# A whole planned order of 4654 tasks rewritten, with the planner's durations changed, in a fused dynamic-convolution and gated-FFN kernel on one core

## The chip, the core and the metric

The kernel runs on one core of one Trainium2 chip. The metric is the device time of one execution in microseconds (us). Beside it stands the profile of one execution: each engine's instructions with their start, length and what released them. The engines are PE (TensorE, matmul; its weight loads are listed apart as PEld), DVE (VectorE), ACT (ScalarE), POOL (GpSimd) and SP (SyncE, which here only issues DMAs). L616 means line 616 of the kernel.

## What is computed

```python
# x: (4, 4160, 192) f32; weight_gen: (4, 4160, 8, 7) f32
w = softmax(weight_gen, axis=-1)                       # 8 heads, 7 taps
a[b, s, h, g] = sum_k w[b, s, h, k] * x_pad[b, s + k, h, g]   # the 7 rows up to s, 24 columns a head
# gated FFN, d_ff = 1024
h = relu(a @ w_in)
c = cw[0] * h[s - 1] + cw[1] * h[s] + cw[2] * h[s + 1]
out = (h * sigmoid(c)) @ w_out
```

## The kernel before

The 16640 rows of the sequence lie as 128 segments of 130 rows, one segment on each of the 128 partitions. The kernel works in 33 blocks of R = 4 rows of every segment. A block goes through these steps, and the names are those of the profile:

- **Products.** POOL multiplies rows of x (tile `ring`) by the softmax weights (tile `w`, two blocks to a group), one tap at a time (L511): four taps into a `px` buffer, three into a `py` buffer. There are three px and two py buffers, used in turn, so block q uses px number q mod 3 and py number q mod 2. In blocks 0 to 2 (PLAN "a") a few products of block 0 are DVE's and TensorE sums all seven products while it transposes them (L554, L565).
- **Folds.** From block 3 on (REST, "d") the products are summed in three steps: `fold1` (L527) is an accumulating DMA that adds the three py pieces to three px pieces, `fold2` (L530) an accumulating DMA that adds px pieces 2, 3 to 0, 1, and `fold3` (L537) a pair of POOL additions of the last two. POOL issues the two DMAs and both use POOL's DMA queue.
- **Softmax of a weight group:** maximum (L447, DVE), subtraction (L450, POOL), exp (L453, ACT), sum (L456, DVE), reciprocal (L465, DVE), product (L472, POOL).
- **Transposes and split.** TensorE transposes the sum (L565), ACT writes its rounded part (`H`, L589), DVE the rest (`L`, and the lower half of `H2`, L593); a small SP transfer copies `H2` to `HB` (L582).
- **Eight units** of 128 of the 1024 hidden columns each: nine matmuls into a PSUM bank `z` (L616), relu (L627, ACT), middle tap of the convolution (L631, ACT), the side taps (L638, DVE, two of them), tanh (L645, ACT), gate product `g` (L654, DVE). ACT carries two rows to the next block (L659).
- **Second matmul** (L675, two blocks later), evacuation (L682, ACT) and store (L686, SP).

Every matmul uses 64 of TensorE's 128 rows; the lower and the upper half work side by side and are planned as two engines, P0 and P8. At the start the weights have to be decoded from f64 bit patterns: chunk by chunk, ACT (L339, L342), four DVE steps (L346, L349, L352, L357), ACT (L860) and DVE (L865), then SP transfers the folded rows (`spread`, L879).

What sets the order: the program first writes down all tasks as (engine, duration, dependences), then takes ORDER, a permutation of the 4654 task numbers, and computes for each task in that order the earliest start that the model allows:

```python
for i in order:
    best[i] = max([best[d] + l_ for d, l_ in preds[i]] + [free.get(u, 0.0) for u in uses[i]] + [0.0])
    for u in uses[i]:
        free[u] = best[i] + dur[i]
seq = [i for i in sorted(range(nt), key=lambda i: (best[i], pos[i])) if tasks[i][3] is not None]
```

The instructions are emitted by rising `best`, so the durations and ORDER together decide only in which order each engine gets its instructions. At run time an engine takes them strictly in that order, and semaphores hold each back until its data are there. Both DMA folds occupy a modelled resource "D" (`dadd`).

Of the kernel before, what the change touches and what calls it, by code (L numbers as in the profile page):

```python
# [36 lines left out]
T_X = (7.4, 11.1)  # L37
T_W = (3.5, 9.5)
# [4 lines left out]
    ("f", 0, 256, 8.2, "VGP", "G"),  # L43
    ("m", 0, 256, 9.0, "VVP", "G"),
    ("f", 256, 512, 11.9, "GVP", "V"),
    ("m", 256, 512, 12.3, "VVP", "G"),
# [225 lines left out]
def kernel(  # L272
# [24 lines left out]
    R = 4  # L297
# [394 lines left out]
    with tc.manual_schedule():  # L692
# [151 lines left out]
        def used(ix):  # L844
            return [k for i in ix for k in last_use[i]]
# [45 lines left out]
        for q in range(2, WB):  # L891
            softmax(q, dma(0.5, spreads[q - 2:q - 1], lambda q=q: load_w(q)))
# [264 lines left out]
```

## Time and profile before

| | us |
|---|---|
| median of 3 runs (lowest, highest) | 695.01 (694.62, 695.83) |
| the profiled execution's own time | 695.11 |
| its span, first to last instruction | 693.4 |
| PE busy | 671.6 |
| DVE busy | 625.2 |
| ACT busy | 610.3 |
| POOL busy | 512.9 |

1.7 us of the profiled execution lie outside its span. A busy TensorE is not TensorE at its peak: its "busy" is the union of both halves, so a stretch in which one half works counts whole, and so does one at half clock. The number of matmuls in a stretch tells more.

### The profile page before, as it was taken

The page shows a single profiled execution, that of the slowest core. Times are in us where ns is not written, and L with a number is a line of the kernel's source. Part 1 is how long each engine was busy: PE and PEld are TensorE (multiplying, and loading weights), DVE is VectorE, ACT ScalarE, POOL GpSimd, SP SyncE. Part 2 cuts the span into 40 slices and gives each one's busy share as a digit, 9 for nine tenths or more (in the row PEclk, how much of TensorE's full clock was granted, in tenths as well). Part 3 has the DMA queues.
Part 4 walks back from the last instruction along what each step waited for, and adds up shares of the span by engine and source line. Part 5 has one row for each costly group of instructions (what it writes and reads, how often), then busy time and mean ns, then how long its engine had stood idle before and what let it go on. Part 6 is the DMA issues. An engine that isn't in the chain of part 4 may idle for free.

```text
span 693.4 us, 17805 instructions
## 1 busy us (share of the span) xinstructions
PE 671.6 (97%) x7177; PEld 652.6 (94%) x7177; DVE 625.2 (90%) x998; ACT 610.3 (88%) x1216; POOL 512.9 (74%) x417
## 2 busy tenths in 40 slices
PE   4899979999999999999999999999999999999998
PEld 3789979999999999999999999999999999999997
DVE  7699968999999999999999999999989998999982
ACT  4489969999999999999999999999999999899972
POOL 6899977989997886959888995798886984731000
PEclk9699989999999999999999999999999999999999
DMA  8728757797888877467977867579858775470101
GB/s 247 212 69 167 160 124 148 157 210 138 181 167 177 165 154 140 97 148 167 202 157 161 182 139 143 111 167 181 183 109 167 138 146 106 89 149 32 33 24 46
DMA packets 38634, 98.79 MB, mean 142 GB/s; under 512 B 3534, under 2 KB 8269, under 8 KB 38552
## 3 DMA queue, kind: packets, MB, share of 16 engines
q0 software_dynamic: 20192, 59.01, 48.6%
q1 hardware_dynamic: 18042, 38.19, 17.4%
q8 instruction: 56, 0.92, 0.5%
q10 hardware_dynamic: 318, 0.46, 0.3%
q14 instruction: 26, 0.21, 0.1%
HBM read 20.51 MB, written 12.78 MB: 48 GB/s over the span
## 4 chain that ended last, share of the span: by engine, by line
PE 80%; POOL 12%; DMA 3%; issue 2%; ACT 1%; DVE 1%; SPq 0%; ACTq 0%; DVEq 0%; POOLq 0%
PE ops L675 39%; PE z L616 36%; POOL px L511 5%; POOL py L511 4%; DMA px<-px 2%; PE tp L565 2%; PE z L675 1%; POOL px L537 1%; POOL px L530 1%; DMA stage<-in_moe_w_in_dram 1%; PE ops L554 1%; POOL w L472 1%; POOL px L527 0%; PE tp L675 0%; PE tp L554 0%
## 5 line engine op out<-in xcount | busy, mean ns | idle before, releaser
L675 PE MATMUL ops<-wo,g 64*128 64x192 f32 x4032 | 575.7, 326 | 0.0
L675 PEld LDWEIGHTS ops<-wo,g 64*128 64x128 f32 x4032 | 537.8, 187 | 6.6 <-ACT o L682 2.5
L616 PE MATMUL z<-H,wi 64*128 64x512 f32 x1716 | 477.6, 425 | 0.5 <-DVE g L654 0.2
L638 DVE SCALAR_TENSOR_TENSOR z<-h,cw,z 128x512 f32<-128x512 f32 (+1 forms) x528 | 379.3, 741 | 24.2 <-ACT z L631 16.8
L616 PEld LDWEIGHTS z<-H,wi 64*128 64x128 f32 x1716 | 292.1, 188 | 5.4 <-DVE g L654 2.2
L511 POOL TENSOR_TENSOR px<-ring,w 128x768 f32<-128x768 f32 (+1 forms) x145 | 234.4, 1870 | 25.7 <-PE tp L565 21.7
L616 PE MATMUL z<-L,wi 64*128 64x512 f32 x528 | 201.9, 395 | 0.0
L654 DVE SCALAR_TENSOR_TENSOR g<-z,h 128x512 f32<-128x512 f32 (+1 forms) x264 | 173.9, 676 | 13.2 <-ACT z L645 11.0
L631 ACT ACTIVATE z<-h,cw 128x512 f32<-128x512 f32 (+1 forms) x264 | 180.4, 685 | 4.5
L627 ACT ACTIVATE h<-z 128x512 f32<-128x512 f32 x264 | 156.7, 595 | 25.8 <-PE z L616 20.5
L511 POOL TENSOR_TENSOR py<-ring,w 128x768 f32<-128x768 f32 (+2 forms) x108 | 167.3, 1759 | 0.0
L645 ACT ACTIVATE z<-z 128x512 f32<-128x512 f32 (+1 forms) x264 | 148.5, 574 | 6.0 <-DVE z L638 5.1
L537 POOL TENSOR_TENSOR px<-px 128x512 f32<-128x512 f32 (+1 forms) x60 | 69.2, 1341 | 46.3 <-DMA px<-px 46.1
L616 PEld LDWEIGHTS z<-L,wi 64*128 64x128 f32 x528 | 97.0, 186 | 1.3
L659 ACT ACTIVATE h<-h 128x512 f32<-128x512 f32 x128 | 79.2, 623 | 0.0
L565 PEld LDWEIGHTS tp<-ident,px 64*128 64x128 f32 x424 | 46.5, 145 | 11.2 <-POOL px L537 6.0
L565 PE MATMUL tp<-ident,px 64*128 64x64 f32 x424 | 49.3, 230 | 7.8 <-POOL px L537 5.1
L589 ACT ACTIVATE H<-tp 64x256 fp32r<-64x256 f32 (+1 forms) x93 | 42.2, 453 | 12.2 <-PE tp L565 8.8
L616 PE MATMUL z<-HB,wi 64*128 64x512 f32 x132 | 52.1, 394 | 0.0
L530 POOL DMA_DIRECT2D px<-px x30 | 42.3, 1409 | 12.5 <-DMA px<-py 12.2
L682 ACT ACTIVATE o<-ops 128x192 f32<-128x192 f32 x126 | 40.8, 323 | 10.5 <-PE ops L675 9.9
L527 POOL DMA_DIRECT2D px<-py x30 | 46.1, 1538 | 4.5 <-POOL py L511 4.5
(80 smaller groups left out, 293.1 us busy)
## 6 DMA issues: line engine op xcount, KB each, us to landing
px<-py POOLq DMA_DIRECT2D x30, 1152.0 KB, 9.9
px<-px POOLq DMA_DIRECT2D x30, 768.0 KB, 7.0
ring<-in_x_dram SPq DMA_DIRECT2D x31, 384.0 KB, 6.2
out_dram<-o SPq DMA_DIRECT2D x31, 384.0 KB, 5.1
HB<-H SPq DMA_DIRECT2D x33, 128.0 KB, 3.0
w<-in_weight_gen_dram SPq DMA_DIRECT2D x15, 224.0 KB, 6.4
r_out<-in_moe_w_out_dram SPq DMA_DIRECT2D x4, 384.0 KB, 4.8
wi<-scr SPq DMA_DIRECT2D x8, 128.0 KB, 5.3
```

Source lines behind the costliest of these rows:

```text
L511: eng.tensor_tensor(out=dst[:, a:b, :].rearrange("p s (h g) -> p s h g", g=GRP), in0=ring[:, p:p + n, :].rearrange("p s (h g) -> p s h g", ...
L530: nc.gpsimd.dma_start(out=fl4(px_b[q % NX][:, 0:2]), in_=fl4(px_b[q % NX][:, 2:4]), accum_op=ALU.add, max_dma_last_dim=3072)
L537: nc.gpsimd.tensor_tensor(out=dst.rearrange("p (s d) -> p s d", s=R), in0=a[:, :, lo:hi], in1=b[:, :, lo:hi], op=ALU.add)
L565: return nc.tensor.matmul(dst[0:D2 if part and i >= 0 else P, c * P + s * H2_:c * P + (s + 1) * H2_], lhsT=src, rhs=ident[r, r], is_transp ...
L616: return [lambda i=i, w=w, nm=nm: nc.tensor.matmul(out=z, lhsT=w[:, fs], rhs=h_t[j, nm][r], start=(not s and i == 0), stop=(s == 1 and i = ...
L627: nc.scalar.activation(out=hrow(f, 2, R), in_=rows(z_t[j, f]), func=ACTF.Relu)
L631: nc.scalar.activation(out=rows(z_t[j, f][:, :no * P]), in_=hrow(f, cc, no), func=ACTF.Copy, scale=cw[:, NF + f:NF + f + 1])
L638: nc.vector.scalar_tensor_tensor(out=z, in0=hrow(f, cc + d, no), scalar=cw[:, k * NF + f:k * NF + f + 1], in1=z, op0=ALU.mult, op1=ALU.add,)
L645: nc.scalar.activation(out=z, in_=z, func=ACTF.Tanh, scale=0.5)
L654: nc.vector.scalar_tensor_tensor(out=rows(g_of(j, f)), in0=rows(z_t[j, f][:, :no * P]), scalar=1.0, in1=hrow(f, cc, no), op0=ALU.add, op1= ...
L659: nc.scalar.activation(out=h[:, f0 // CG, 0:2].rearrange("p s f t -> p (s f t)"), in_=h[:, f0 // CG, R:R + 2].rearrange("p s f t -> p (s f ...
L675: return nc.tensor.matmul(out=hold[0][2][:, 0:D], lhsT=g_of(j, n)[r, c], rhs=wo[r, n, :], start=(first and n == 0), stop=(last and n == NF ...
```

## The change

ORDER is replaced as a whole. The modelled durations and landing times change with it: first arrivals of x and w (T_X, T_W), arrivals of the weight chunks (CH), issue times and landing times of loads and stores, POOL's time to issue a fold, transposes, splits and the matmul step. No instruction's work changes, and no buffer.

```diff
-T_X = (7.4, 11.1)
-T_W = (3.5, 9.5)
+T_X = (8.2, 11.7)
+T_W = (3.5, 10.3)
...
-    ("f", 0, 256, 8.2, "VGP", "G"),
-    ("m", 0, 256, 9.0, "VVP", "G"),
-    ("f", 256, 512, 11.9, "GVP", "V"),
-    ("m", 256, 512, 12.3, "VVP", "G"),
+    ("f", 0, 256, 9.2, "VGP", "G"),
+    ("m", 0, 256, 9.8, "VVP", "G"),
+    ("f", 256, 512, 13.1, "GVP", "V"),
+    ("m", 256, 512, 14.3, "VVP", "G"),
...
-    "0 1 6 15 24 33 44 53 64 384 4 385 2 5 3 7 8 9 10 11 12 13 14 25 27 131 28 132 133 34 29 26 36 35 134 30 148 37 "
...
-        m_late = dma(0.5, [], lambda: load_in(nc.sync, *CH[4][:3]))
-        x_t_[2] = dma(0.5, [], lambda: load_x(2 * R - 1, 2 * R + 3))
+        m_late = dma(2.3, [], lambda: load_in(nc.sync, *CH[4][:3]))
+        x_t_[2] = dma(1.8, [], lambda: load_x(2 * R - 1, 2 * R + 3), 4.5)
...
-            softmax(q, dma(0.5, spreads[q - 2:q - 1], lambda q=q: load_w(q)))
+            softmax(q, dma(1.0, spreads[q - 2:q - 1], lambda q=q: load_w(q), 4.5))
...
-                x_t_[q] = dma(1.2, all_taps.get(q - RB, []), lambda: load_x(R * q - 1, R * q + 3), 8.0)
+                x_t_[q] = dma(1.8, all_taps.get(q - RB, []), lambda: load_x(R * q - 1, R * q + 3), 8.0)
...
-                a_ = dadd([prod[i] for i in (0, 1, 2, 4, 5, 6)], 6.5, lambda: fold1(q), 0.82)
+                a_ = dadd([prod[i] for i in (0, 1, 2, 4, 5, 6)], 6.5, lambda: fold1(q), 1.3)
...
-                    a_ = dadd([a_, prod[3]], 4.4, lambda: fold2(q), 0.775)
+                    a_ = dadd([a_, prod[3]], 4.4, lambda: fold2(q), 1.0)
...
-                            f_ = task("P8" if s else "P0", 0.06 * nc_, [e_] + after,
-                                      [(0.06, lambda n=n, c=c, s=s, one=one: one(n, c, s)) for c in range(nc_)])
+                            f_ = task("P8" if s else "P0", 0.07 * nc_, [e_] + after,
+                                      [(0.07, lambda n=n, c=c, s=s, one=one: one(n, c, s)) for c in range(nc_)])
...
-                a_ = task("A", 0.56 if pr else 0.49, [f_] + hd, lambda part=part, pr=pr: split_hi(q, part, hold[part], pr))
-                l_ = task("V", 0.78 if pr else 0.6, [a_], lambda part=part, pr=pr: split_lo(q, part, hold[part], pr))
+                a_ = task("A", 0.74 if pr else 0.49, [f_] + hd, lambda part=part, pr=pr: split_hi(q, part, hold[part], pr))
+                l_ = task("V", 0.89 if pr else 0.6, [a_], lambda part=part, pr=pr: split_lo(q, part, hold[part], pr))
...
-                stored.append(dma(1.2, [e_], lambda: store(j, 0, no)))
+                stored.append(dma(1.8, [e_], lambda: store(j, 0, no)))
```

What the new table does to the engines' orders is seen in three places.

**First place: POOL, the folds of blocks 4 and 5.** px1 belongs to block 4, px2 and py1 to block 5, px0 to block 6 (and, in fold3, still to block 3). Before:

```order
L537 TENSOR_TENSOR px0_95<-px0_95 128x256
L511 TENSOR_TENSOR py1_99<-ring_82,w3_90 128x768 x2
L527 DMA px2_97<-py1_99 128x3x768
L530 DMA px1_96<-px1_96 128x2x768
L511 TENSOR_TENSOR px2_97<-ring_82,w3_90 128x768
L450 TENSOR_TENSOR w0_87<-w0_87,m0_91 128x448
L450 TENSOR_TENSOR w1_88<-w1_88,m1_93 128x448
L511 TENSOR_TENSOR px0_95<-ring_82,w3_90 128x768 x3
L537 TENSOR_TENSOR px1_96<-px1_96 128x512
```

With the change:

```order
L537 TENSOR_TENSOR px0_95<-px0_95 128x256
L511 TENSOR_TENSOR px2_97<-ring_82,w3_90 128x192
L511 TENSOR_TENSOR px2_97<-ring_82,w3_90 128x576
L511 TENSOR_TENSOR px2_97<-ring_82,w3_90 128x768
L511 TENSOR_TENSOR py1_99<-ring_82,w3_90 128x768
L530 DMA px1_96<-px1_96 128x2x768
L511 TENSOR_TENSOR py1_99<-ring_82,w3_90 128x768 x2
L527 DMA px2_97<-py1_99 128x3x768
L511 TENSOR_TENSOR px2_97<-ring_82,w3_90 128x768
L511 TENSOR_TENSOR px0_95<-ring_82,w3_90 128x768
L537 TENSOR_TENSOR px1_96<-px1_96 128x512
```

fold2 of block 4 (L530 on px1) stood behind fold1 of block 5 (L527 on px2) and now stands ahead of it, with two products between them; the two subtractions L450 of the weight groups 4 and 5 have gone forward, to either side of fold1 of block 4. The next two pairs (blocks 5 and 6, 6 and 7) are exchanged in the same way; the two after them already stood so before.

**Second place: DVE at the start.** dps_224 and dps_228 are the second weight chunk, dps_274 and dps_276 the third, tp and ops the transposed block 0. Before:

```order
L511 TENSOR_TENSOR px0_95<-ring_82,z1_109 128x768
L357 ISA dps_224<-dps_224,scr1_114 128x512
L865 TENSOR_TENSOR wi_79<-dps_224,wi_79 128x256
L346 TENSOR_SCALAR dps_274<-dps_274 128x256
L349 TENSOR_SCALAR scr0_113<-dps_274 128x256
L352 SCALAR_TENSOR_TENSOR dps_274<-dps_274,scr0_113 128x256
L357 ISA dps_274<-dps_274,scr0_113 128x512
L593 TENSOR_TENSOR L1_0_101<-tp_190,H1_0_100 128x512
L865 TENSOR_TENSOR scr0_113<-dps_274,scr0_113 128x256
L593 TENSOR_TENSOR H2_0_102<-ops_176,H2_0_102 64x512
```

With the change:

```order
L511 TENSOR_TENSOR px0_95<-ring_82,z1_109 128x768
L349 TENSOR_SCALAR scr1_114<-dps_228 128x256
L352 SCALAR_TENSOR_TENSOR dps_228<-dps_228,scr1_114 128x256
L357 ISA dps_228<-dps_228,scr1_114 128x512
L593 TENSOR_TENSOR L1_0_101<-tp_190,H1_0_100 128x512
L865 TENSOR_TENSOR wi_79<-dps_228,wi_79 128x256
L593 TENSOR_TENSOR H2_0_102<-ops_179,H2_0_102 64x512
L346 TENSOR_SCALAR dps_276<-dps_276 128x256
```

Both splits (L593) of block 0 now stand ahead of the four decode steps of the third chunk; before they stood behind them.

**Third place: TensorE, the first unit.** tp_190 and ops_ are the banks of block 0, tp_289 and tp_281 that of block 1, z1 the bank of the first unit. Before:

```order
L554 MATMUL tp_190<-ident_76,px0_95 128x128 x4
L565 MATMUL tp_289<-ident_76,px1_96 128x64 x12
L565 MATMUL ops_312<-ident_76,px1_96 64x64
L616 MATMUL z1_109<-H1_0_100,wi_79 128x512
L565 MATMUL ops_312<-ident_76,px1_96 64x64 x3
L616 MATMUL z1_109<-H1_0_100,wi_79 128x512
```

With the change:

```order
L554 MATMUL ops_179<-ident_76,px0_95 64x128 x4
L565 MATMUL tp_281<-ident_76,px1_96 128x64 x4
L616 MATMUL z1_109<-H1_0_100,wi_79 128x512 x2
L616 MATMUL z1_109<-H2_0_102,wi_79 128x512 x2
L616 MATMUL z1_109<-L1_0_101,wi_79 128x512
L565 MATMUL tp_281<-ident_76,px1_96 128x64 x3
```

The first unit's matmuls start behind four transposes of block 1 in place of thirteen. In block 0 the transposes into the `tp` bank now end ahead of those into the `ops` bank.

## Rows read from the trace of the kernel before

**Rows 1.** Two lines of the page's 40 slices: busy tenths, granted clock in tenths
```profile
PE   4899979999999999999999999999999999999998
...
PEclk9699989999999999999999999999999999999999
```

**Rows 2.** Windows: length; PE, PEld, DVE, ACT, POOL busy (instructions); clock, DMA
```profile
80.00:100.00 20.00, 15.64 (x157) 15.09 (x155) 14.67 (x24) 14.41 (x29) 15.28 (x13) 0.90 0.71 145
240.00:260.00 20.00, 20.00 (x223) 19.83 (x221) 19.20 (x31) 18.77 (x39) 16.34 (x13) 1.00 0.67 137
```

**Rows 3.** Waits of TensorE: for whom, us in total, times, longest
```profile
PE tp L565 <- POOL px L537: 5.1, 2, 4.4
PE tp L565 <- DVE L L593: 2.7, 1, 2.7
```

**Rows 4.** Windows of 4 us, same columns
```profile
24.00:28.00 4.00, 4.00 (x31) 3.13 (x31) 0.95 (x2) 1.21 (x3) 4.00 (x4) 0.50 0.67 185
52.00:56.00 4.00, 3.91 (x30) 3.32 (x28) 3.97 (x9) 3.94 (x9) 4.00 (x4) 1.00 0.88 202
92.00:96.00 4.00, 0.53 (x5) 0.23 (x3) 3.18 (x5) 2.22 (x5) 0.43 (x1) 0.98 0.87 221
96.00:100.00 4.00, 3.11 (x24) 3.02 (x25) 0.34 (x1) 0.97 (x2) 4.00 (x4) 0.50 0.14 55
100.00:104.00 4.00, 4.00 (x34) 3.85 (x32) 3.65 (x6) 2.84 (x6) 4.00 (x5) 0.67 0.01 2
104.00:108.00 4.00, 4.00 (x46) 4.00 (x44) 2.37 (x5) 3.07 (x7) 4.00 (x5) 1.00 0.89 152
```

**Rows 5.** TensorE's timeline: start, length, instruction, idle time before it and releaser
```profile
21.16 1.19 PE L565 MATMUL tp<-ident,px 64*128 64x64 f32 x9 [2.75 <-DVE L L593]
22.43 0.77 PE L616 MATMUL z<-H,wi 64*128 64x512 f32 x1
...
96.89 0.37 PE L565 MATMUL tp<-ident,px 64*128 64x64 f32 x1 [4.36 <-POOL px L537]
...
140.88 0.27 PE L565 MATMUL tp<-ident,px 64*128 64x64 f32 x1 [0.72 <-POOL px L537]
```

**Rows 6.** POOL's timeline around the folds of blocks 3 to 5
```profile
46.13 0.98 POOL L450 TENSOR_TENSOR w<-w,m 128x448 f32<-128x448 f32 x1
47.06 4.57 POOL L511 TENSOR_TENSOR py<-ring,w 128x768 f32<-128x768 f32 x3
51.94 1.31 POOL L527 DMA_DIRECT2D px<-py  x1 [0.31 <-POOL py L511]
...
66.91 2.23 POOL L527 DMA_DIRECT2D px<-py  x1
...
80.69 1.29 POOL L527 DMA_DIRECT2D px<-py  x1 [0.30 <-POOL py L511]
81.49 1.72 POOL L530 DMA_DIRECT2D px<-px  x1
...
95.57 1.94 POOL L537 TENSOR_TENSOR px<-px 128x512 f32<-128x512 f32 x2 [4.43 <-DMA px<-px]
```

**Rows 7.** DMA issues in 60:64, 66:68, 83:95, 118:130: count, KB each, us to landing
```profile
px<-px POOLq DMA_DIRECT2D x1, 768.0 KB, 7.1
...
px<-py POOLq DMA_DIRECT2D x1, 1152.0 KB, 12.2
...
px<-px POOLq DMA_DIRECT2D x1, 768.0 KB, 14.0
...
px<-px POOLq DMA_DIRECT2D x1, 768.0 KB, 8.7
```

**Rows 8.** DVE's timeline at the start
```profile
18.50 0.43 DVE L346 TENSOR_SCALAR dps<-dps 128x256 f32<-128x256 f32 x1 [0.98 <-ACT dps L339]
...
20.34 0.68 DVE L593 TENSOR_TENSOR L<-tp,H 128x512 fp32r<-128x512 f32 x1
...
28.22 0.49 DVE L638 SCALAR_TENSOR_TENSOR z<-h,cw,z 128x256 f32<-128x256 f32 x1 [2.48 <-ACT z L631]
```

More of the change, by code (lines that the diff above doesn't have):

```diff
@@ L898 @@
                 wo[:, 2 * c:2 * c + 2].rearrange("p c d -> p (c d)").bitcast(I32), r_out[c],
-                slots[iB][:, 0:w], slots[iC][:, 0:w], dma(1.6, spreads, lambda c=c: load_out(c)), used((iB, iC)), WOE[c],
+                slots[iB][:, 0:w], slots[iC][:, 0:w], dma(1.8, spreads, lambda c=c: load_out(c), 4.0), used((iB, iC)), WOE[c],
             )
@@ L918, in loads @@
                 g0 = 2 * (g - WB)
-                softmax(g, dma(0.7, all_taps[g0] + (all_taps[g0 - 1] if g0 else []), lambda: load_w(g), 9.0))
+                softmax(g, dma(1.0, all_taps[g0] + (all_taps[g0 - 1] if g0 else []), lambda: load_w(g), 9.0))
         def head(q):
@@ L994, in unit @@
             k_ = 4 if late(j, f) else 5
-            a_ = task("P0", 0.231 * k_, deps_, (k_, lambda: mm1(j, f, 0)), after=[last_mm[0]] + ([] if n else zfirst))
-            mm[n] = task("P8", 0.231 * (9 - k_), [a_] + (twins[j] if late(j, f) else []), (9 - k_, lambda: mm1(j, f, 1)),
+            a_ = task("P0", 0.233 * k_, deps_, (k_, lambda: mm1(j, f, 0)), after=[last_mm[0]] + ([] if n else zfirst))
+            mm[n] = task("P8", 0.233 * (9 - k_), [a_] + (twins[j] if late(j, f) else []), (9 - k_, lambda: mm1(j, f, 1)),
                          after=[last_mm[1]])
@@ L1097, in one @@
                     return made[n]()
-                ms = [(0.231, lambda n=n, one=one: one(n)) for n in range(fn[0])]
+                ms = [(0.233, lambda n=n, one=one: one(n)) for n in range(fn[0])]
             else:
```

403 rows, old and new, of the table ORDER are left out of this document.

## The prediction, made before the changed kernel ran

> **What bounds the kernel now.** I read the slices of the page first. TensorE is busy in nine tenths or more of nearly every slice, with a hole in the second and third slice and one in the sixth, and the clock line falls at the same places [rows 1]. The windows of 20 us say what "busy" is worth: a steady stretch holds 223 matmuls in 20 us, that is 11.1 a us, with TensorE at 20.00 and DVE at 19.20 of 20 us; the stretch from 80 to 100 us holds only 157 [rows 2]. So from about 104 us to the end the kernel runs at TensorE's own rate, and a new order can win nothing there: TensorE's work is the same. What can be won lies ahead of it.
>
> The waits of TensorE then name two places: one of 4.4 us for POOL's fold3 and one of 2.7 us for DVE's split [rows 3]. The windows of 4 us show what the first costs. From 92 to 104 us they hold 5, 24 and 34 matmuls, where 46 stand in the one behind them, and the clock is 0.50 (1.2 of 2.4 GHz) in 96 to 100 us, 0.67 in the next and full from 104 on [rows 4]. TensorE's timeline has the gap: 4.36 us up to 96.89, released by L537 of POOL, which is fold3 of block 4 [rows 5].
>
> POOL's timeline tells why fold3 is late. fold1 of block 5 is issued at 80.69 and fold2 of block 4 behind it at 81.49; fold3 of block 4 stands for 4.43 us and starts at 95.57 [rows 6]. The DMA table gives that fold2 14.0 us from issue to landing, where a fold2 with none just ahead of it took 7.1 and one later 8.7 [rows 7]. So the wait is a queue: a fold of 768 KB behind one of 1152 KB that nobody needs yet.
>
> At the start DVE does the split of block 0 at 20.34, behind four decode steps that begin at 18.50 [rows 8]; TensorE waits for it up to 21.16, and its first unit begins at 22.43 [rows 5] at half clock (0.50 in the window from 24 us [rows 4]). DVE itself then waits 2.48 us for that unit, up to 28.22 [rows 8], and is full in the 50s (3.97 of 4 us [rows 4]).
>
> **The change, term by term**, against the profiled execution's own 695.1 us (the median of the runs shown is 695.0, so they can stand for each other). A measurement of this kernel can tell about 0.2%, 1.4 us, from no change.
>
> *Folds of blocks 4 and 5.* When does fold2 of block 4 land now? Before, 81.49 − 51.94 = 29.55 us lay between the issues of fold1 of block 3 and fold2 of block 4, all of it POOL's own work but for 0.3 us of waiting [rows 6]. By the new order two products (4.57 / 3 = 1.5 us each) and the issue of fold1 of block 5 (81.49 − 80.69 = 0.8, with 0.3 idle ahead) leave this stretch, and two subtractions of 0.98 come in: 29.55 − 3.0 − 1.1 + 2.0 = 27.4. So fold2 is issued at 51.94 + 27.4 = 79.3, or a little earlier if POOL gets to block 3 sooner. It lands 7.1 to 8.7 us later, at 86.4 to 88.0, and fold3 (1.94) ends at 88.3 to 89.9, in place of 97.5. fold1 of block 4 has to land first: before it was issued at 66.91, and one subtraction more and two short products less ahead of it leave it about there, 12.4 us ahead of fold2; its landing took 12.2 [rows 7], so it is just there in time. TensorE ran out of work 4.36 us before 96.89, at 92.5. The cover is 2.6 to 4.2 us, and the gap closes. At the dear end fold2 takes 14.0 in its new place too: it lands at 93.3, fold3 ends at 95.2, and a gap of 2.7 us stays.
>
> What the gap cost: 4.36 us idle, and half of the 5.7 us that it took to get the clock back (96.9 to about 102.6: a mean of 0.67 in the window from 100 us is 2.6 of its 4 us at 0.50 and the rest at full [rows 4]), 2.85: 7.2 together. By count, 63 matmuls stand in the three windows from 92 us for 135 at the steady rate; 72 / 11.1 = 6.5. I take **6.8**; the low end is 7.2 − 2.7 − 2.85 = 1.6, with a gap left and the clock falling in it. What is late next? fold1 of block 5 now comes about 3.8 us behind the new fold2; fold2 of block 5 is again ahead of the next fold1, and TensorE wants block 5 some 19 us after block 4 with POOL working 16.3 of 20 us [rows 2], so I see no second gap there.
>
> On transfers, the Trainium skill (DMA: Bandwidth & Descriptors, Anatomy of one DMA) gives a fit of 2.0 us plus the bytes at 436 GB/s; an estimate by that page is 3.8 us for fold2 and 4.7 for fold1. By it fold2 would have landed by 90 us behind fold1 too, TensorE would not have starved, and the exchange would be worth nothing, which would leave the sum at 692.4. The rows say 7.1 alone and 14.0 in the queue [rows 7], so the measurement decides, and the page's figure is not used.
>
> *The start.* DVE's two splits of block 0 go ahead of the four decode steps, 20.34 − 18.50 = 1.84 us [rows 8], and TensorE's first unit stands behind 4 transposes, not 13. So the first unit can be through some 2 us sooner, and DVE's convolution of it falls into DVE's idle 2.48 us. From there to about 70 us DVE is nearly full, so what DVE gains is what the start gains. Bounds: nothing, if the third chunk (whose decode now comes behind the splits) or POOL's products for block 1 hold the second unit where it is; 3.4 us, if DVE's idle 2.48 and most of 0.98 [rows 8] are both filled. I take **2.0**, nearer the rows of DVE's idle time.
>
> *A small gap of block 6.* TensorE's 0.72 us at 140.88 is the same wait for fold3 [rows 5]; with its fold2 ahead of the next fold1 it should go: **0.7** (0 to 0.7).
>
> *Everything else.* In the steady stretch the halves are interleaved anew and some softmax steps move by a unit or two. That costs nothing as long as TensorE's rate holds, which covers it: DVE has 0.8 us of room in 20 [rows 2]. I take 0, and treat the loss of this cover as a rival. DMA issue times in the model change no instruction.
>
> Sum: 695.1 − 6.8 − 2.0 − 0.7 = **685.6 us**.
>
> **The rivals.**
>
> *The start gains nothing* (chance 0.17). For it: TensorE is at half clock there [rows 4], and the third chunk's decode is later than before. Against: DVE's idle time. Time: 695.1 − 6.8 − 0.7 = 687.6.
>
> *The gap closes only in part* (0.13): fold2 lands as late as 14.0 us after its issue because loads and stores of SP's queue share the engines, or POOL stands at the subtraction of group 5, whose maximum DVE must now deliver earlier. For it: DVE is full in that stretch [rows 4]. Against: 7.1 to 8.7 where no fold is just ahead. Time: 695.1 − 1.6 − 2.0 − 0.7 = 690.8.
>
> *The exchange does nothing, as by the page's fit* (0.03): something other than the fold held fold3. Against: 14.0 [rows 7] and the releaser named [rows 6]. Time: 695.1 − 2.0 − 0.7 = 692.4.
>
> *Slower: DVE's queue loses its room in the steady stretch* (0.08). Place: the 26 blocks or so between 160 and 660 us. A block takes about 19.4 us (eight units); DVE has 0.8 us of room in 20. If the new interleaving lets DVE stand for ACT or TensorE by more than this room, each further 0.1 us a block costs 2.6 us in all. It decides at 9.5 / 26 = 0.37 us a block beyond the room: from there on the kernel is slower than before. With 0.5 us it would be 685.6 + 13 = 698.6. For it: the order is new everywhere, and room is small. Against: TensorE's neighbours stood so near the limit before and TensorE was still at 20.00 of 20 [rows 2].
>
> **How the numbers follow.** The forecast has 0.59, the rivals 0.17, 0.13, 0.03 and 0.08. The range runs from 682.5 (a full 3.4 and 7.2 with the 0.7 is 683.8, and a little for holes in the early windows that I have not priced) to 691.5, which takes in the first two rivals: outside are the last two and about 0.05 below, together under 0.2. Faster by over 0.2% (below 693.7): all but the slower rival and a small part of the others, 0.89. Within 0.2%: 0.04. Slower: 0.07.
>
> **What would show it.** Right: no wait of TensorE for L537 above 1 us; the fold2 of the first blocks lands in 6 to 9 us; the clock is full from the start's recovery on, with no fall near 96 us; windows from 92 to 104 us hold about 45 matmuls per 4 us; the first L638 of DVE comes at 25 to 26.5, and TensorE's first unit at 19.5 to 21. The steady windows still hold 222 or so. Wrong: a new wait of TensorE of over 3 us with a fall of the clock behind it, or steady windows of under 220 matmuls with DVE idle in them.

## The result, and the profile after

The changed kernel takes **686.28 us** (median of 4 runs, 685.49 to 687.13) beside 694.82 for the kernel before: a ratio of 0.9875, 95% interval 0.9858 to 0.9892, or 8.5 us less. Forecast were 685.6, 682.5 to 691.5. The span of the profiled execution is 684.6 us, 8.8 less. A second measurement, run beside e5 to e7, gave 685.33 with 694.85 for before (below).

The page of after, the lines that answer to [rows 1]:

```profile
span 684.6 us, 17785 instructions
...
PE   4889999999999999999999999999999999999998
...
PEclk9899999999999999999999999999999999999999
```

The dip in the sixth slice (87 to 104 us) is gone, in the busy line and in the clock. The waits of TensorE, as in [rows 3]:

```profile
PE tp L831 <- DVE h L357: 7.7, 1, 7.7
PE ops L565 <- DVE H L593: 1.8, 1, 1.8
PE ops L554 <- POOL px L511: 1.7, 1, 1.7
PE z L616 <- DMA wi<-scr: 1.7, 1, 1.7
PE tp L565 <- DVE L L593: 0.6, 1, 0.6
```

No wait for fold3 (L537) is left; the wait for the split (L593 of L) has shrunk from 2.7 to 0.6, but two others stand at the start now, 1.7 for a transfer of weights and 1.8 for another split. (The 7.7 comes before there is anything to compute.) POOL's timeline, as in [rows 6]:

```profile
63.98 1.66 POOL L530 DMA_DIRECT2D px<-px  x1
...
67.52 1.88 POOL L527 DMA_DIRECT2D px<-py  x1
...
79.31 2.05 POOL L530 DMA_DIRECT2D px<-px  x1
80.09 4.36 POOL L511 TENSOR_TENSOR py<-ring,w 128x768 f32<-128x768 f32 x2
84.74 1.29 POOL L527 DMA_DIRECT2D px<-py  x1 [0.30 <-POOL py L511]
85.56 3.54 POOL L511 TENSOR_TENSOR px<-ring,w 128x768 f32<-128x768 f32 x2
88.57 2.44 POOL L537 TENSOR_TENSOR px<-px 128x512 f32<-128x512 f32 x2
```

fold2 of block 4 goes out at 79.31, where 79.3 was forecast, and fold1 of block 5 behind it at 84.74. Of DMA issues in 79 to 83 us, as in [rows 7], the fold2 has:

```profile
px<-px POOLq DMA_DIRECT2D x1, 768.0 KB, 7.8
```

It lands 7.8 us later, at 87.1, where it took 14.0 before, and fold3 starts at 88.57 without a wait. Windows of 4 us, as in [rows 4], at the fold and at the start:

```profile
20.00:24.00 4.00, 2.31 (x10) 1.83 (x10) 2.84 (x7) 1.19 (x4) 4.00 (x4) 0.69 0.40 99
24.00:28.00 4.00, 4.00 (x45) 3.30 (x43) 2.23 (x7) 1.70 (x4) 2.67 (x2) 0.50 0.68 142
28.00:32.00 4.00, 4.00 (x57) 3.59 (x56) 3.54 (x7) 1.80 (x4) 3.43 (x3) 0.96 0.92 297
...
36.00:40.00 4.00, 2.60 (x29) 2.38 (x31) 3.94 (x9) 2.95 (x8) 3.38 (x3) 0.82 0.54 142
40.00:44.00 4.00, 4.00 (x43) 3.72 (x41) 3.93 (x10) 2.79 (x9) 4.00 (x4) 0.75 0.00 0
...
92.00:96.00 4.00, 4.00 (x49) 3.93 (x47) 3.57 (x6) 3.97 (x8) 4.00 (x4) 1.00 0.80 200
96.00:100.00 4.00, 4.00 (x48) 3.71 (x46) 3.73 (x7) 3.67 (x8) 4.00 (x4) 1.00 0.51 90
100.00:104.00 4.00, 4.00 (x46) 4.00 (x44) 3.89 (x8) 3.93 (x10) 3.70 (x4) 1.00 1.00 174
...
240.00:260.00 20.00, 20.00 (x225) 19.72 (x222) 19.45 (x32) 19.36 (x40) 15.51 (x13) 1.00 0.69 149
```

Where 5, 24 and 34 matmuls stood there are 49, 48 and 46, at full clock; the steady window holds 225 (223 before). At the start things are less clear: the clock is back at 28, but TensorE then runs dry at 36 to 40 us and the clock falls once more.

VectorE's timeline of the start, as in [rows 8]:

```profile
18.22 0.69 DVE L593 TENSOR_TENSOR L<-tp,H 128x512 fp32r<-128x512 f32 x1 [1.78 <-ACT H L589]
...
26.63 1.01 DVE L638 SCALAR_TENSOR_TENSOR z<-h,cw,z 128x256 f32<-128x256 f32 x2 [1.56 <-ACT z L631]
```

The split is 2.1 us earlier and the first convolution 1.6, but in this profile VectorE's waiting is split in two rather than filled.

**Where the time goes.** A unit's relu (L627 on ScalarE) marks how far the kernel is. Its start for the first unit of block 3, of block 4 and of block 6, read from ScalarE's timelines:

| kernel | block 3 | block 4 | block 6 | block 3 to 6 |
|---|---|---|---|---|
| before | 88.83 | 113.31 | 153.19 | 64.36 |
| after | 88.83 | 107.68 | 144.90 | 56.07 |
| after, again | 87.59 | 106.44 | 143.63 | 56.04 |
| pairs (e1) | 89.61 | 107.26 | 145.99 | 56.38 |
| one pair (e2) | 89.15 | 106.80 | 148.19 | 59.04 |
| gap filled (e4) | 88.33 | 109.69 | 151.20 | 62.87 |
| pairs, splits ahead (e5) | 87.95 | 105.50 | 144.25 | 56.30 |
| e5 and 8 matmuls (e10) | 89.30 | 106.94 | 145.74 | 56.44 |
| pairs, start filled (e11) | 86.95 | 104.51 | 143.22 | 56.27 |

From block 3 to block 6 the change saves 8.3 us, and two executions of it agree within 0.03. Behind block 6 the distance hardly alters (8.0 at block 10). Up to block 3 this one pair of profiles shows no gain at all, where 2.0 were forecast. That had to be tested, and so had the 8.3.

### The profile page after: what moved, and what is told of

It reads as the page before. It is cut to its first block, busy times and chain, and to the rows that moved or that the text cites. A ratio compares the mean times of both kernels' runs of the same rounds, so it can differ in the third digit from the quotient of the medians.

```text
span 684.6 us, 17785 instructions
## 1 busy us (share of the span) xinstructions
PE 667.1 (97%) x7177; PEld 649.9 (95%) x7177; DVE 626.0 (91%) x998; ACT 611.0 (89%) x1216; POOL 513.2 (75%) x417
## 4 chain that ended last, share of the span: by engine, by line
PE 94%; DMA 2%; DVE 2%; ACT 1%; issue 0%; SPq 0%; ACTq 0%; DVEq 0%
PE ops L675 45%; PE z L616 44%; PE tp L565 2%; PE z L675 1%; DMA wi<-scr 1%; DMA ring<-in_x_dram 1%; PE tp L675 1%; DVE z L638 0%; PE ops L565 0%; DVE dps L346 0%; ACT h L627 0%; DVE dps L357 0%; DVE dps L352 0%; ACT dps L339 0%; DVE scr L349 0%
## 5 line engine op out<-in xcount | busy, mean ns | idle before, releaser
L675 PEld LDWEIGHTS ops<-wo,g 64*128 64x128 f32 x4032 | 532.3, 187 | 5.6 <-ACT o L682 2.0
L616 PE MATMUL z<-H,wi 64*128 64x512 f32 x1716 | 470.9, 423 | 2.1 <-DMA wi<-scr 1.7
L511 POOL TENSOR_TENSOR px<-ring,w 128x768 f32<-128x768 f32 (+1 forms) x145 | 226.5, 1795 | 3.1 <-DMA ring<-in_x_dram 1.6
L627 ACT ACTIVATE h<-z 128x512 f32<-128x512 f32 x264 | 156.6, 593 | 21.7 <-PE z L616 18.2
L511 POOL TENSOR_TENSOR py<-ring,w 128x768 f32<-128x768 f32 (+2 forms) x108 | 170.9, 1829 | 0.0
L537 POOL TENSOR_TENSOR px<-px 128x512 f32<-128x512 f32 (+1 forms) x60 | 69.4, 1348 | 12.8 <-DMA px<-px 12.7
L530 POOL DMA_DIRECT2D px<-px x30 | 41.1, 1371 | 34.2 <-DMA px<-py 34.2
L527 POOL DMA_DIRECT2D px<-py x30 | 47.3, 1576 | 6.2 <-POOL py L511 6.2
L565 PE MATMUL tp<-ident,px 64*128 64x64 f32 x424 | 47.6, 224 | 0.6 <-DVE L L593 0.6
```

Of the source, the lines that this page charges most:

```text
L511: eng.tensor_tensor(out=dst[:, a:b, :].rearrange("p s (h g) -> p s h g", g=GRP), in0=ring[:, p:p + n, :].rearrange("p s (h g) -> p s h g", ...
L527: nc.gpsimd.dma_start(out=fl4(px_b[q % NX][:, 0:3]), in_=fl4(py_b[q % NY][:, 0:3]), accum_op=ALU.add, max_dma_last_dim=3072)
L537: nc.gpsimd.tensor_tensor(out=dst.rearrange("p (s d) -> p s d", s=R), in0=a[:, :, lo:hi], in1=b[:, :, lo:hi], op=ALU.add)
L565: return nc.tensor.matmul(dst[0:D2 if part and i >= 0 else P, c * P + s * H2_:c * P + (s + 1) * H2_], lhsT=src, rhs=ident[r, r], is_transp ...
L616: return [lambda i=i, w=w, nm=nm: nc.tensor.matmul(out=z, lhsT=w[:, fs], rhs=h_t[j, nm][r], start=(not s and i == 0), stop=(s == 1 and i = ...
L627: nc.scalar.activation(out=hrow(f, 2, R), in_=rows(z_t[j, f]), func=ACTF.Relu)
```

## The experiments

In each, the order is computed as in the kernel and single entries are then moved; the numbers of lines behind these edits shift by up to 7 (L627 is L632 in two of them).

**The folds' order alone: e1, e2, e3.** e1 and e2 are the kernel before with pairs exchanged, e3 is the kernel after with them put back.

```diff
+        for q in (4, 5, 6):        # e2: (4,)
+            i, k = fold_of[q, 2], fold_of[q + 1, 1]
+            best[i], pos[i] = best[k], pos[k] - 0.5        # e3: + 0.5
         seq = [i for i in sorted(range(nt), key=lambda i: (best[i], pos[i])) if tasks[i][3] is not None]
```

e1. Expected:

> The kernel before with one thing of the change alone: for blocks 4, 5 and 6 the second fold is issued just ahead of the next block's first fold, the rest of the order stays. Fold theory (the gain comes from block 4's second fold landing in time, and the later start of the kernel gave nothing): no wait for L537 above 1 us, full clock from 92 to 104, and 686.5 to 687.5 us, that is 7.3 to 8.3 of the 8.5 that the whole change gave. Rival (the new plan as a whole is what pays, the pairs alone shift the wait to another fold or to VectorE): 690 or more.

Measured: 687.96 us, ratio 0.9894 (0.9878 to 0.9911), 7.2 less than before. TensorE's waits in e1, beside one of 10.1 at the very start:

```profile
PE tp L565 <- DVE L L593: 2.7, 1, 2.7
PE z L616 <- DVE g L654: 0.3, 1, 0.3
```

The wait for the split stands as before and that for fold3 is gone; three entries of the table do 7.2 of the 8.5. It is a little above the expected 687.5, since the start gives something after all (below).

e2. Expected:

> The kernel before with one exchange alone, that of block 4's second fold with block 5's first. Fold theory: the 4.36 of the wait and the half clock behind it go, the 0.72 at 140.88 stays: 687.3 to 688.5 us, about 7 below before. Rival (block 5's first fold, now behind it in the queue, is late in its turn and block 5 waits): 690 or more with a new wait between 104 and 125.

Measured: 689.67 us, ratio 0.9924 (0.9909 to 0.9938), 5.4 less. Up to block 4's first unit it is e1's equal (17.65 us from block 3's in both, 24.48 before: 6.8 less). Then POOL's timeline shows where some of it goes back:

```profile
97.96 1.87 POOL L527 DMA_DIRECT2D px<-py  x1
98.75 2.33 POOL L530 DMA_DIRECT2D px<-px  x1
...
113.13 1.95 POOL L537 TENSOR_TENSOR px<-px 128x512 f32<-128x512 f32 x2 [3.00 <-DMA px<-px]
```

TensorE's timeline has the gap behind it, 1.4 us:

```profile
114.45 0.34 PE L565 MATMUL tp<-ident,px 64*128 64x64 f32 x2 [1.39 <-POOL px L537]
```

Before, TensorE came to block 5 too late to notice that this fold2 was behind a fold1 as well. The time lies between the two expected ranges. The rival was right in kind (block 5 waits), though it is block 5's own fold2 that is late, not its fold1. Once block 4 doesn't wait, the pairs of blocks 5 and 6 are worth 2.7 us (59.04 against 56.38); what they would be worth while it does was not run, but TensorE's waits for them in the kernel before are 0.7 in all.

e3. Expected:

> The changed kernel with the three pairs put back, each second fold just behind the next block's first fold. Fold theory: the wait for L537 of 4 to 5 us near 92 to 97 and the half clock behind it come back, 693 to 695 us. Rival (the rest of the new order has slack of its own for the fold): below 690.

Measured: 708.46 us, ratio 1.0193 (1.0178 to 1.0208): 13 us slower than before and 22 slower than after. Neither theory had that. POOL's timeline of e3:

```profile
82.29 1.29 POOL L527 DMA_DIRECT2D px<-py  x1 [0.30 <-POOL py L511]
83.08 1.72 POOL L530 DMA_DIRECT2D px<-px  x1
...
98.90 1.94 POOL L537 TENSOR_TENSOR px<-px 128x512 f32<-128x512 f32 x2 [11.01 <-DMA px<-px]
...
123.47 1.94 POOL L537 TENSOR_TENSOR px<-px 128x512 f32<-128x512 f32 x2 [8.29 <-DMA px<-px]
...
147.78 1.94 POOL L537 TENSOR_TENSOR px<-px 128x512 f32<-128x512 f32 x2 [8.97 <-DMA px<-px]
```

The DMA issues of 82 to 84 us:

```profile
px<-py POOLq DMA_DIRECT2D x1, 1152.0 KB, 11.6
px<-px POOLq DMA_DIRECT2D x1, 768.0 KB, 15.7
```

The new order has only two products between the fold1 in question and fold3. With the queue turned round, POOL, which works through its instructions in order, stands 8 to 11 us at each of three fold3s, and TensorE waits 16.0 us in all for them. An early fold3 pays only with an early fold2; with the old order in the queue it is 13 us worse than the old kernel.

The two folds take about the same time either way. In e3 they are issued from 82.29 and are both down at 83.08 + 15.7 = 98.8, 16.5 us later. In e1, fold2 first, they are issued at 79.50 and 81.22 and land 7.8 and 14.4 us after that, the last at 95.6, 16.1 us after the first issue:

```profile
px<-py POOLq DMA_DIRECT2D x1, 1152.0 KB, 14.4
px<-px POOLq DMA_DIRECT2D x1, 768.0 KB, 7.8
```

Over all such pairs up to 200 us in these traces it is 13.8 to 16.5 us with fold1 first and 14.4 to 16.2 with fold2 first. Order only says which comes first. The Trainium skill (DMA: Bandwidth & Descriptors, Queues, rings and completion order) says of the queues of SP and ScalarE that a DMA engine consumes one ring's descriptors in order; POOL's 61 transfers land in the order of their issue in every trace here.

**What the half clock behind the gap costs: e4**, the kernel before with 18 matmuls in block 4's gap.

```diff
+                        if q == 4 and part == 0:
+                            for _ in range(18):
+                                nc.tensor.matmul(
+                                    out=hold[0], lhsT=wh[0:H2_, 0, 0:P], rhs=h_t[3, "H1"][0:H2_], start=True, stop=True,
...
                     i, end = out_[n][0], n == len(out_) - 1 and c == nc_ - 1
```

> The kernel before with 18 matmuls more ahead of block 4's first transposes (operands that are there, a target that the transposes overwrite; the output is unchanged), about 4.2 us of TensorE at 0.233 each, so that they stand in the gap of 4.36. It splits the gain: if the half clock that follows the gap costs what the prediction says (2.85), the clock stays full from 96 to 104, and the time is 692 to 692.5. Rival (the clock behind the gap costs nothing, since those rows wait for something else, or the added matmuls come too late to fill the gap): 694.5 to 695.5.

Measured: 694.05 us (10 runs), ratio 0.9986 (0.9977 to 0.9995), 1.1 less: between the two. The windows of e4 say why.

```profile
92.00:96.00 4.00, 4.00 (x20) 3.02 (x19) 2.68 (x5) 1.75 (x4) 1.35 (x2) 1.00 0.88 235
96.00:100.00 4.00, 4.00 (x50) 3.85 (x51) 2.09 (x4) 2.72 (x6) 4.00 (x4) 1.00 0.04 17
100.00:104.00 4.00, 4.00 (x48) 4.00 (x47) 3.75 (x7) 3.58 (x9) 4.00 (x5) 1.00 0.09 18
...
116.00:120.00 4.00, 2.53 (x32) 2.53 (x34) 2.16 (x4) 2.30 (x5) 3.55 (x4) 1.00 0.61 197
```

The clock stays full, and by block 4's first unit 3.1 us are saved (21.36 against 24.48 from block 3's), where the prediction had 2.85 for the half clock. At block 5 TensorE, now earlier, waits 1.54 us for a fold3 that came forward by only 1.5 us (from 29.31 to 27.82 behind block 3's first unit), and half of it is gone again. So the half clock behind the gap costs about what it was said to cost, and a saving lasts only if the next fold comes earlier too.

**The start: e5**, the three pairs, and block 0's two splits with ScalarE's copies ahead of the third chunk's decode.

```diff
+        t = best[ids['dec', 3]]
+        for part in (0, 1):
...
+            best[ids['hi', 0, part]] = best[ids['dec', 3] - 2] - 2e-4 + 1e-4 * part
+            best[ids['lo', 0, part]] = t - 2e-4 + 1e-4 * part
```

> The kernel with only the three pairs exchanged (687.96 us), and beside that block 0's two splits, with the ScalarE copies ahead of them, put in front of the third chunk's decode, as the change has them; nothing else. The prediction's step says that this is worth 2.0: 685.5 to 686.5 us. Theory after the traces (VectorE has the same work to do up to block 3's first unit whatever comes first, and its idle time of 7.3 us between 8 and 72 us is not less but elsewhere): the first unit's h comes up to 2 us earlier, block 3's first unit does not, and the time is 687 to 689 us.

Measured: 686.30 us, ratio 0.9874 (0.9858 to 0.9891): 1.7 less than e1 (the intervals of the two ratios overlap), and no different from the whole change. That is the prediction's step, not the theory that I had formed from one pair of traces, and that theory falls. Its evidence was too thin: kernels with one and the same start reach block 3 at 88.33 to 89.61 (before, e1, e2, e4), so one profile against one profile says nothing within a microsecond. VectorE's first convolution starts at 27.72 here, behind a wait of 0.57, and in e1 at 28.79, behind one of 3.15. Where TensorE's clock differs is seen in the windows of e1 (with the old start)

```profile
20.00:24.00 4.00, 1.97 (x24) 2.00 (x26) 3.73 (x9) 1.33 (x4) 4.00 (x4) 0.82 0.75 192
24.00:28.00 4.00, 4.00 (x28) 3.04 (x26) 1.50 (x4) 0.73 (x2) 4.00 (x4) 0.50 0.72 187
28.00:32.00 4.00, 4.00 (x33) 3.40 (x32) 3.11 (x6) 2.45 (x6) 1.40 (x1) 0.50 1.00 334
32.00:36.00 4.00, 4.00 (x57) 3.79 (x55) 3.21 (x7) 2.10 (x5) 3.75 (x3) 0.50 0.12 47
36.00:40.00 4.00, 4.00 (x40) 3.38 (x37) 3.21 (x7) 2.81 (x7) 4.00 (x4) 0.98 0.36 92
```

and of e5:

```profile
20.00:24.00 4.00, 3.41 (x36) 2.95 (x37) 3.18 (x7) 1.33 (x5) 4.00 (x4) 0.80 0.83 196
24.00:28.00 4.00, 3.59 (x26) 2.71 (x25) 2.88 (x7) 2.33 (x6) 2.36 (x3) 0.50 0.61 146
28.00:32.00 4.00, 3.88 (x25) 2.97 (x26) 3.77 (x8) 1.83 (x5) 3.65 (x3) 0.50 0.95 290
32.00:36.00 4.00, 4.00 (x70) 3.65 (x68) 3.63 (x8) 2.62 (x6) 4.00 (x4) 0.92 0.50 170
```

Taking 1 minus the clock over the windows, e1 loses (0.18 + 0.50 + 0.50 + 0.50 + 0.02) x 4 = 6.8 us of TensorE's full speed, e5 (0.20 + 0.50 + 0.50 + 0.08) x 4 = 5.1. The other profiles with the old start lose 6.8 too, and those with the new order's 5.1, after itself among them (1.28 x 4, in two pieces). That is the profiled executions; one of e5's other three has the mean clock of e1's runs, 0.989, and took 686.34 all the same.

**Does VectorE, or GpSimd, pace the start? e6, e7, and after once more.** e6 leaves out the clamp in the weights' decode, e7 moves two maxima.

```diff
-                    t_ = task("V", vec(N), [t_], st[k])
+                    t_ = task("V", vec(N), [t_], st[k] if k > 2 else None)        # e6
...
+        for g, n in ((2, 0), (3, 2)):        # e7
+            best[ids['max', g]] = best[ids['conv', 0, FORD[n]]] - 1e-4
```

> The changed kernel without the clamp step of the weights' decode (L346, 11 instructions, about 5 us of VectorE, 4 us of it behind the first 16 us); the saturation of weights beyond the format's range is left out. Theory that VectorE paces the kernel up to block 3's first unit: that unit comes 2 to 4 us earlier than at 88.8 and the time falls by as much, 682 to 684.5 us. Rival that GpSimd's products and folds pace it (fold3 of block 3 at 72.6): 685.5 to 687.

> The changed kernel with two maxima of the softmax (L447 of groups 2 and 3) put ahead in VectorE's queue: group 2's ahead of the first unit's convolution, into VectorE's 1.56 us of waiting there, group 3's by three instructions. GpSimd's two waits of 1.90 and 1.65 us for them go. Theory that VectorE paces the start: GpSimd runs ahead by up to 3 us and block 3's first unit by 0.6 at most, 685.5 to 686.5 us. Rival that GpSimd paces it: 683 to 684.5.

> The changed kernel unaltered, as the base of the other three on the same chip: 685.5 to 687 us, and block 3's first unit within 1 us of 88.8, which says how far one profile's start stands from another's.

Measured: e6 684.63 us (682.63 to 685.35, ratio 0.9849, 0.9831 to 0.9866), e7 685.33 (0.9864, 0.9849 to 0.9879), after again 685.33 (0.9864, 0.9849 to 0.9879). What e6 leaves out is this group of VectorE in 8 to 72 us of after:

```profile
L346 DVE TENSOR_SCALAR dps<-dps 128x256 f32<-128x256 f32 (+2 forms) x9 | 4.6, 514 | 0.6 <-ACT dps L339 0.6
```

4.6 us less work for VectorE brought 0.7 by the medians, not to be told from nothing by the intervals; block 3's first unit came at 86.69, 0.9 ahead of after once more's and 2.1 ahead of after's. In e7 GpSimd waits 0.40 us for a maximum and 1.12 for a reciprocal, where it waited 1.90 and 1.65 for maxima in after and 2.61 in after once more; the time is that of after once more to the hundredth. So nothing shows GpSimd pacing the start. Both times lie between the two expected ranges, and within 0.2 us of that of the theory of VectorE: a part for VectorE stays possible, but not microsecond for microsecond. In after once more VectorE's first convolution starts at 24.54 with no wait ahead of it, where after had 26.63 and 1.56:

```profile
24.54 1.02 DVE L638 SCALAR_TENSOR_TENSOR z<-h,cw,z 128x256 f32<-128x256 f32 x2
```

VectorE's idle time does tell where the start stands. In the window from 8 to 72 us it is 64 less the busy time, and it follows block 3's first unit: 7.3 in before, 7.1 and 5.8 in after's two profiles, 8.5 in e1 and 6.3 in e5. Block 3's start less this idle time is 81.1 to 81.9 in all profiles but e6's, which has less work (78.1).

**Is it the half clock? e8 to e11.** They add matmuls at the start that keep TensorE busy, and leave the output as it is.

```diff
+            for _ in range({(0, 0, 0, 2): 9, (0, 3, 0, 0): 10}.get((j, f, s, i), 0)):        # e8; e9, e11: {(0, 3, 0, 0): 12}
+                nc.tensor.matmul(
+                    out=z_b[3], lhsT=wh[r, 0, 0:P], rhs=h_t[0, "H1"][r], start=True, stop=True, skip_group_check=True)
...
+                        if q == 1 and part == 0:        # e9, e10, e11
+                            for _ in range(8):
+                                nc.tensor.matmul(
...
```

e8 is after with both of its sets, e9 is e5 with 8 and 12, e10 is e5 with the 8 alone, e11 is e1 (no splits ahead) with 8 and 12.

> The changed kernel with 19 matmuls more at the start (operands that are there, a PSUM target that is free; the output is unchanged): 9 in the first unit ahead of its third matmul, where TensorE waits 1.7 us for a transfer, and 10 ahead of the second unit's first, so that TensorE stands idle less. All five starts in the new order, and that with the splits alone, lose 5.1 us to a granted clock below full between 20 and 44 us (the sum of 1 minus clock over the windows), the old order 6.8. Theory that the half clock is what holds the start back: the loss falls below 3 and the time by 1.5 to 3, 682.5 to 684 us. Rival that VectorE's and ScalarE's chain on the weights holds it and a faster TensorE only waits: the loss may fall, but idle time comes in its place, 685 to 686.5 us.

> The order of before with the three pairs exchanged and the splits ahead (686.30 us), with 8 matmuls more ahead of block 1's first transposes, in TensorE's gap of 1.5 us, and 12 ahead of the second unit's first matmul. Half clock theory: 682.5 to 684.5 us, block 3's first unit 2 us earlier than the 88.0 without the added ones. Rival: 686 to 687.

> The same with the 8 matmuls alone, without the 12. They close the gap ahead of the first unit and not the wait ahead of the second: the clock falls some microseconds later than before or not for as long. Half clock theory: between the other two, 684 to 686 us. Rival: 686 to 687.

> The kernel with the three pairs exchanged (687.96 us) and the same 8 and 12 matmuls more at the start, without the splits ahead. It tells apart what the splits' move is worth: runs of the kernels so far with the same order but another loss to the half clock at the start (6.8 against 5.1) differ by 1.4 to 2.0 us, and at a loss of 0 nothing more is gained. If the splits' move pays only by a shorter stretch at half clock, this kernel, with the clock kept up in the old order, is as fast as that with the splits moved: 685.5 to 686.7 us, block 3's first unit at 87.7 to 88.3. If the splits' place itself counts, the added matmuls give nothing here: 687.3 to 688.3 us and block 3's first unit at 89 or later.

Measured: e8 684.85 us (684.16 to 686.23), ratio 0.9877 (0.9855 to 0.9898). e9 688.0 (685.53 to 692.51), 0.9925 (0.9894 to 0.9955). e10 687.33 (684.96 to 687.71), 0.9897 (0.9878 to 0.9917). e11 686.82 (685.11 to 692.76), 0.9914 (0.9881 to 0.9947). e9's and e10's medians lie above both expected ranges, and e8's and e11's between them. The runs of e9 and e11 fall apart: three of eight and two of six stand at 692 with a mean clock of 0.988, and of the others all but one, at 689.3, between 685.1 and 687.3 with a mean clock of 1.00; what happens in the former was not profiled and stays open. The windows of e11, first and last of four that are all alike in this:

```profile
20.00:24.00 4.00, 4.00 (x42) 3.35 (x41) 3.63 (x9) 1.17 (x3) 4.00 (x4) 1.00 0.98 234
...
32.00:36.00 4.00, 4.00 (x62) 3.50 (x59) 3.79 (x8) 3.07 (x8) 4.00 (x4) 1.00 0.24 62
```

In e8, e9 and e11 the clock never falls at the start. Put by loss, block 3's first unit starts as follows:

- 6.8 lost (before, e1, e2, e4, e10): 88.33 to 89.61, mean 89.0
- 5.1 lost (after twice, e3, e5, e7; e6, with less work, left out): 87.59 to 88.83, mean 88.0
- nothing lost (e8, e9, e11): 86.63 to 87.72, mean 87.1

e10 is the telling one: with the splits ahead, but with 6.8 lost, it is back at 89.30 and 687.33. Within its own runs the two with a mean clock of 0.994 took 684.96 and 685.78, the four at 0.989 and 0.992 687.2 to 687.7. And e11, without the splits ahead but with nothing lost, is earlier than e9, which has them ahead (86.95 and 87.72). VectorE's idle time goes along: 8.05 in e10, 5.33 in e11. So by these profiles the splits' move pays by the shorter stretch at half clock; the first two groups of the list overlap, and the run of e5 at 0.989 speaks against it.

Of the next 5.1 us of loss only about 1 comes back at block 3 by the means: 0.2 from e5 to e9, 1.6 from after's two to e8. Why not more is open. The added matmuls take some 0.23 us each themselves, 4.4 in e8, partly outside the gaps; and TensorE still stands idle for 2.0 of the 24 us from 20 to 44 in e8, but for 0.25 in e11. The time of e8 lies between its two theories: its three runs at a mean clock of 1.00 took 684.16 to 684.85, the two at 0.994 686.15 and 686.23. The kernel before, run beside these without added matmuls, shows the same kind of price: 695.26 and 695.34 at 0.985, 692.04 at 0.994 and 692.28 at 0.998, that is some 3 us for 6 to 9 of TensorE's full speed. The Trainium skill (TensorE: Matmul & The Clock Gate, HAM oscillation) counts the throttled time times 1 minus 1.2/2.4 as the penalty, which is the loss as summed here; these runs show it as an upper bound, not as the time to be had.

## Why the prediction was right, point by point

**The folds: right, 8.0 (e1, from block 3 to block 6) to 8.3 for 7.5.** That fold2 waits behind a fold1 in POOL's queue, and that the exchange ends this, is shown by e1 and e3. The issue at 79.3, the landing in 7.1 to 8.7 us and the 45 or more matmuls from 92 to 104 us came as forecast. Block 4's term was 6.8 and measured 6.8 (e2 at block 4), with the half clock's part of 2.85 at 3.1 (e4). "A small gap of block 6", 0.7, was priced too low: with block 4 on time, the pairs of blocks 5 and 6 are worth 2.7 of e1's 8.0, and 1.4 of that is a wait that before did not show. The terms don't add up as rows of before suggest, but the sum was off by only 0.8. Three readings in the working were slightly off and changed nothing: at 11.15 matmuls a us the 12 us hold 134, not 135, so the count gives 6.4, not 6.5; fold1 of block 5 came 5.4 us behind the new fold2, not 3.8; and the fold2 that took 8.7 (issued at 128.15) was not alone, a fold1 issued at 121.92 was still on its way until 131.4.

**The start: the gain is there, about 1 for 2.0, and the working says only half of why.** What the two measurements of the whole change leave beside the 8.3 is 0.2 and 1.2; e1 to e5 is 1.7 by the medians, and the means by loss give 1.0. The step was that the first unit's convolution falls into VectorE's idle 2.48 us, and that "what DVE gains is what the start gains". The second half holds: block 3's first unit moves with VectorE's idle time in all these kernels but e6, 1.6 us less idle and 1.2 us earlier from before to after once more, 0.2 and nothing in after's first profile. The first half is not sure: that execution of after still waits 1.56 ahead of the convolution and 1.78 at the split, the other not at all and 0.98. How much of VectorE's waiting goes depends on how long TensorE is at half clock, which the prediction named only in a rival: with the splits moved but 6.8 lost little is gained (e10: 687.33, e1: 687.96), and with nothing lost they need not be moved (e11). Of the signs named, the convolution at 25 to 26.5 came at 26.63 and 24.54; TensorE's first unit began at 19.30, for 19.5 to 21, but stood 1.69 us in the middle of it for a transfer of weights; and the clock, which was to stay full once it was back, fell a second time (0.82 in the window from 36 us, 0.75 in the next). What paces the start beyond the clock is not settled: by the medians GpSimd's relief gave nothing, VectorE's 0.7 and TensorE's 0.5 to 1.4. Relieving two at once was not tried.

**The rest: right.** Everything else was taken as nothing. e5, two moves of the many in the new order, takes 686.30; after takes 686.28 and 685.33. The slower rival (VectorE's room in the steady stretch) did not come: 225 matmuls in the window, with VectorE at 19.45 of 20. "The exchange does nothing" and "closes only in part" are out by e1.

The forecast's 685.6 lies between the two measurements, 686.28 and 685.33, with one term up to 0.8 too small and one about 1 too large: that they cancel is luck.

## What to carry to other kernels

In these traces transfers of one queue land in the order of issue, so when work waits for a transfer, look first at what stands ahead of it in its queue that nobody needs yet; three exchanged entries gave most of what an order written anew gave. On an engine that works in order, move an instruction that waits for a transfer ahead only if the transfer comes ahead too (e3 lost 22 us), and expect that removing the first late transfer shows the next (e2, e4). Before a small term is called nothing, see how far two executions of the same kernel differ at that place: here 1.2 us at 88 us, and 0.03 us over the stretch behind it.

## What was not expected of the hardware

A half clock that costs 5.1 us of TensorE's speed by the windows was taken away with 19 added matmuls of no use, and 0.5 to 1.4 us came back by the medians. Eight added matmuls that closed the gap ahead of the first unit only (e10) did not help: in the profile the clock fell in the same window of 20 to 24 us all the same (0.83 against 0.80) and stayed at half for longer, through the window from 32 us, as it does with the old start. That they made it worse is not shown, since two of e10's six runs have a mean clock of 0.994, and one of e5's four has 0.989. And a pair of folds of 1152 and 768 KB takes about 15 us (13.8 to 16.5) whichever goes first.
